# Scaling the attention output instead of its weights for four pairs, two compose tiles, an early second pair and six narrow FFN blocks

## Chip, core and metric

The kernel runs on one core of a Trainium2 chip. The metric is the device time of one execution in microseconds (us). TensorE (PE) multiplies matrices, VectorE (DVE), ScalarE (ACT) and GpSimd (POOL) work on elements, SyncE (SP) issues most transfers.

## What is computed

Three layers, one behind the other, on 2304 tokens of width 512:

```python
# attention, per head (4 batches, 8 heads, 576 tokens, head size 64)
decay = cum[:, :, :, None] - cum[:, :, None, :]      # cum = cumsum(log(clip(f)))
scores = where(causal, -1e9, q @ k.T / sqrt(D) + decay)
attn = exp(scores - max(scores)); attn = attn / (sum(attn) + 1e-9)
x = attn @ v
# FFN, float64 weights, d_ff 2048
h = x @ w_in
g = where(h >= 1, h, where(h <= -1, 0, (h + 1) ** 2 / 4))
x = g @ w_out
# top-1 mixture of 8 experts (d_ff 1024): gate by normalised dot products
out = gate * (max(x @ w1[e], 0) @ w2[e])
```

## The kernel before

**Order.** The instruction order of all engines is made when the program is built. Every step of the work is a Python generator that yields resources (`Buffers`), events and uses of an engine (`Use`, with a planned duration and a priority); `Order` plays these through and emits the instructions in the order that comes out. On the chip each engine then runs its own list strictly in order. What the plan got wrong in a duration shows on the chip as a wait.

**Attention.** Two heads make a pair, four pairs a batch, sixteen pairs in all. `load` brings q and k of a pair, VectorE transposes them (`turned`), and `unit` handles one of five query blocks (c = 4 is the last 64 queries of both heads in one block, then 3, 2, 1, 0): TensorE writes scores into a bank `SR` or `SRx`, VectorE adds the decay and the mask and takes the extreme (L588), ScalarE takes the exponential and its row sum (L593), VectorE turns the sum into its inverse (L598, L600), GpSimd scales P with it (L604), TensorE transposes P into a bank `T` (L618), ScalarE or VectorE copies that into `pt`, and `weighted` multiplies with v: the burst `X`, and `U` for the last 64 queries. For the first four pairs (`NSUM`) the decay comes from TensorE itself, by one more matmul (`sums`), and the mask from a fixed tile `past`; later pairs load a decay tile `cm`/`cl` for each pair, from a table `rows`. From pair 4 on `SRx` belongs to the FFN.

**Filler.** `keep_warm` issues matmuls of the identity (`warm`) wherever the plan has TensorE idle, until the first attention outputs are in place.

**FFN, first half.** The float64 weights arrive in 16 pieces of 512 KB (w_in and w_out in turn). `float64_piece` composes float32 values from the integer halves in a tile `wx` (one buffer): ScalarE absolute value, VectorE a maximum (L830), a shift (L832) and two merges (L834, L836), ScalarE the rounded high part, GpSimd the rest. The hidden layer is split into eight groups of 128; each takes twelve matmuls into a bank (`hp`, L886), then the activation, then twelve matmuls of the second layer (`accp`, L1020). Tokens go in blocks: `NARROW` = 5 blocks of 256, which start as soon as their attention pairs are there and mix with the rest of the attention, and then two blocks of 512. The second half of the FFN (`hr`) and the experts (`hm`) follow.

## Time and profile before

| | us |
|---|---|
| median of 3 runs | 861.24 (859.62 to 863.11) |
| profiled execution | 862.92 |
| its span, first to last instruction | 861.3 |

How to read it: the span is cut into stages, since the engines' shares change. TensorE is busy nearly throughout, but its filler counts as busy, so the filler's own records and the idle time per stage must be read with it. A lower granted clock (a share of full speed) marks stretches in which TensorE was slowed.

### The profile page before, as it was taken

The page shows a single profiled execution, that of the slowest core. Times are in us where ns is not written, and L with a number is a line of the kernel's source. Part 1 is how long each engine was busy: PE and PEld are TensorE (multiplying, and loading weights), DVE is VectorE, ACT ScalarE, POOL GpSimd, SP SyncE. Part 2 cuts the span into 40 slices and gives each one's busy share as a digit, 9 for nine tenths or more (in the row PEclk, how much of TensorE's full clock was granted, in tenths as well). Part 3 has the DMA queues.
Part 4 walks back from the last instruction along what each step waited for, and adds up shares of the span by engine and source line. Part 5 has one row for each costly group of instructions (what it writes and reads, how often), then busy time and mean ns, then how long its engine had stood idle before and what let it go on. Part 6 is the DMA issues. An engine that isn't in the chain of part 4 may idle for free.

```text
span 861.3 us, 14317 instructions
## 1 busy us (share of the span) xinstructions
PE 840.4 (98%) x5000; PEld 672.7 (78%) x5000; DVE 463.9 (54%) x1112; ACT 361.9 (42%) x845; POOL 306.4 (36%) x407
## 2 busy tenths in 40 slices
...
GB/s 139 184 183 182 167 159 145 139 135 108 113 67 118 78 103 134 74 75 171 117 127 49 73 123 159 189 191 123 147 123 73 50 50 50 263 103 50 98 74 25
DMA packets 152264, 101.91 MB, mean 118 GB/s; under 512 B 102866, under 2 KB 121810, under 8 KB 152192
## 3 DMA queue, kind: packets, MB, share of 16 engines
...
## 4 chain that ended last, share of the span: by engine, by line
PE 83%; DVE 7%; POOL 2%; issue 2%; DMA 2%; ACT 2%; SPq 0%; ACTq 0%; DVEq 0%; POOLq 0%
PE hm L886 12%; PE hr L886 12%; PE hp L886 9%; PE accp L1020 6%; PE accr L1020 6%; PE accBr L1020 6%; PE accm L1032 6%; PE accBm L1032 6%; PE SR L538 4%; PE T L618 4%; PE X L658 4%; PE gt L1236 1%; PE U L711 1%; PE SR L533 1%; PE T_None L618 1%
## 5 line engine op out<-in xcount | busy, mean ns | idle before, releaser
L908 POOL TENSOR_TENSOR glr<-gr,ghr 128x512 fp32r<-128x512 f32 x36 | 48.3, 1341 | 141.7 <-PE accBr L1020 69.1
L604 POOL TENSOR_SCALAR P<-P,st 128x512 f32<-128x512 f32 (+3 forms) x128 | 76.9, 615 | 38.8 <-DVE st L600 25.4
L886 PE MATMUL hr<-rx,wb 128*128 128x512 f32 (+1 forms) x384 | 90.1, 368 | 0.2 <-DVE rx L872 0.2
L886 PE MATMUL hm<-mx,wm 128*128 128x512 f32 (+1 forms) x336 | 87.0, 379 | 0.0
L593 ACT ACTIVATE P<-P,st 128x512 f32<-128x512 f32 (+3 forms) x128 | 71.4, 559 | 32.9 <-DVE st L588 31.8
L917 DVE SCALAR_TENSOR_TENSOR glm<-hm,ghm 128x512 fp32r<-128x512 f32 x36 | 24.8, 689 | 103.5 <-PE accBm L1032 68.4
L916 ACT ACTIVATE ghm<-hm 128x512 fp32r<-128x512 f32 x36 | 21.6, 599 | 132.9 <-PE accBm L1032 120.6
L886 PEld LDWEIGHTS hr<-rx,wb 128*128 128x128 f32 x384 | 65.5, 188 | 14.0 <-DVE rx L872 0.6
L886 PEld LDWEIGHTS hm<-mx,wm 128*128 128x128 f32 x336 | 61.0, 188 | 14.9 <-issue 3.4
L908 POOL TENSOR_TENSOR glp<-gp,ghp 128x512 fp32r<-128x512 f32 x36 | 49.8, 1383 | 55.1 <-ACT ghp L907 48.2
L1020 PE MATMUL accp<-ghp,wa 128*128 128x256 f32 (+1 forms) x384 | 68.8, 307 | 0.0
L588 DVE CUSTOM_DVE_ANT_0 P<-SR,cm 128x512 f32<-128x512 f32 (+3 forms) x96 | 45.1, 484 | 24.8 <-PE SR L538 22.5
L1020 PEld LDWEIGHTS accp<-ghp,wa 128*128 128x128 f32 x384 | 53.9, 190 | 5.3 <-issue 2.2
L618 PE MATMUL T<-ident,P 128*128 128x128 f32 x320 | 52.5, 278 | 3.5 <-POOL P L604 2.9
L638 ACT COPY pt<-T 128x512 f32<-128x512 f32 (+2 forms) x96 | 35.3, 391 | 35.9 <-PE T L618 35.2
L902 DVE SCALAR_TENSOR_TENSOR gr<-tr 128x512 f32<-128x512 f32 x36 | 25.9, 721 | 42.6 <-POOL glr L908 31.7
L618 PEld LDWEIGHTS T<-ident,P 128*128 128x128 f32 x320 | 36.7, 141 | 14.9 <-POOL P L604 6.5
L538 PE MATMUL SR<-kt,qt 64*128 64x384 f32 (+3 forms) x224 | 44.9, 478 | 3.0 <-DVE st L588 2.9
L1020 PE MATMUL accr<-ghr,wb 128*128 128x512 f32 (+1 forms) x160 | 47.0, 375 | 0.0
L1020 PE MATMUL accBr<-ghr,wb 128*128 128x512 f32 (+1 forms) x160 | 46.5, 372 | 0.0
L1032 PE MATMUL accm<-wm,ghm 128*128 128x512 f32 x144 | 46.2, 394 | 0.0
L1032 PE MATMUL accBm<-wm,ghm 128*128 128x512 f32 x144 | 45.8, 392 | 0.0
...
## 6 DMA issues: line engine op xcount, KB each, us to landing
...
```

The costliest lines, as they stand in the source:

```text
L538: nc.tensor.matmul(bank[:, j, :w], qt[p, P * c:P * c + P], kt[p, :w], start=True, stop=i >= NSUM)
L588: yield dve(w + 80, lambda: nc.vector.tensor_tensor_reduce(out=pv_, in0=so, in1=m, scale=-0.125, scalar=3e38, op0=ALU.add, op1=ALU.min, ac ...
L593: yield act(w, lambda: nc.scalar.activation(pw, pw, AF.Exp, bias=st[:, n:n + 1], scale=-1.0, accum_out=st[:, 2 + n:3 + n]), 1, 330)
L604: yield pool1(w, lambda: nc.gpsimd.tensor_scalar(pw, pw, st[:, 6 + n:7 + n], 1.0, ALU.mult, ALU.mult), 0)
L618: nc.tensor.transpose(T[:, P * n:P * n + P], p[:, P * kb:P * kb + P], ident)
L638: yield act(n, lambda: nc.scalar.copy(dh, src), 0)
L658: nc.tensor.matmul(X[D * j:D * j + D, P * kb:], vt[:, kb, j], pt[i, j][0][:, 512 * kb:512 * kb + 512 - P * kb], start=(kb == 0), stop=(kb ...
L886: nc.tensor.matmul(oo, a[:, c, cs], x[c], start=(ip == 0 and c == 0), stop=(ip == 2 and c == KC - 1))
L902: yield dve(n, lambda: nc.vector.scalar_tensor_tensor(g, t, 0.5, t, ALU.min, ALU.mult), 2)
L908: yield pool2(n, lambda: nc.gpsimd.tensor_tensor(gl, g, f32(gh), ALU.subtract), 1)
L1020: nc.tensor.matmul(acc[d][:, :w], b[:, fc, P * d:P * d + P], g, start=(fc == 0 and ip == 0 and (not narrow or d % 2 == 0)), stop=(fc == NF ...
L1032: nc.tensor.matmul(acc[a * (4 // na)], g[:, P * a:P * a + P], b[:, fc], start=(fc == 0 and ip == 0), stop=(fc == NF - 1 and ip == 2))
```

## The change

For the first four pairs P isn't scaled for the query blocks 3 to 0. The row sums of a pair go into one tile `tot` of 128 x 8. Once all eight are there, the new `shares` takes the inverse on VectorE and TensorE spreads it by eight matmuls with the identity into a bank R (the FFN's hidden bank, free at that time), laid out as X is. ScalarE copies R, and VectorE multiplies X with it into `xT`. Block 4 is scaled as before.

The compose tile gets two buffers until all 16 pieces are through (the second one lies in the attention's pool), and the maximum of the first nine pieces goes to GpSimd. The loads of the second pair no longer wait for the running sum. `NARROW` is 6, so the first FFN half has six blocks of 256, one of 512 and one of 256 in the wide layout.

```diff
+NMAX = 9
-    NARROW = 5
+    NARROW = 6
     FIRST = [(TB * n, TB) for n in range(NARROW)] + [
-        (t, 2 * TB) for t in range(TB * NARROW, NT, 2 * TB)]
+        (t, min(2 * TB, NT - t)) for t in range(TB * NARROW, NT, 2 * TB)]
...
-        if i:
+        if i == 1:
+            yield raw_ok[0, "k"]
+        elif i:
             yield sums_there
-        t = yield dma(P * S * 6, lambda: put({"q": q, "k": k}[n], n), 4 if i else 0.5, k=4)
+        t = yield dma(P * S * 6, lambda: put({"q": q, "k": k}[n], n),
+                      4 if i > 1 else 0.5, k=4)
...
+        late_sum = i < NSUM and c < 4
+        total = sums_of[i][:, c, n:n + 1] if late_sum else st[:, 2 + n:3 + n]
         yield act(w, lambda: nc.scalar.activation(pw, pw, AF.Exp, bias=st[:, n:n + 1], scale=-1.0,
-                                                  accum_out=st[:, 2 + n:3 + n]), 1, 330)
+                                                  accum_out=total), 1, 330)
         done(summed)
-        if n == 0:
+        if late_sum:
+            done(all_summed[i])
+        elif n == 0:
...
-        yield pool1(w, lambda: nc.gpsimd.tensor_scalar(pw, pw, st[:, 6 + n:7 + n], 1.0, ALU.mult,
-                                                       ALU.mult), 0)
+        if not late_sum:
+            yield pool1(w, lambda: nc.gpsimd.tensor_scalar(pw, pw, st[:, 6 + n:7 + n], 1.0,
+                                                           ALU.mult, ALU.mult), 0)
...
+    def shares(i):
+        yield all_summed[i]
+        tot = sums_of[i].rearrange("p c j -> p (c j)")
+        inv = ap.tile([P, 4, 2], F32, tag="inv", name=f"inv{i}", bufs=2)
+        yield Use("DVE", 150, lambda: nc.vector.tensor_scalar(tot, tot, 1e-9, None, ALU.add), 0)
+        yield Use("DVE", 150, lambda: nc.vector.reciprocal(inv.rearrange("p c j -> p (c j)"), tot), 0)
+        gh_ = yield (h_b, 1)
+        R = hidden_bank(f"R{i}", 0)
+        def spread():
+            for c in range(4):
+                for j in range(2):
+                    nc.tensor.matmul(R[D * j:D * j + D, P * c:P * c + P],
+                                     inv[:, c, j:j + 1].to_broadcast([P, D]), ident,
+                                     start=True, stop=True)
+        yield Use("PE", mm(P, 8), spread, 0.9)
...
-        yield act(512, lambda: nc.scalar.copy(xT[:, :512], X), 0)
+        if i < NSUM:
+            yield share[i]
+            R, gh_ = share[i].t
+            yield act(512, lambda: nc.scalar.copy(xT[:, :512], R), 0)
+            give(h_b, gh_)
+            yield dve(512, lambda: nc.vector.tensor_tensor(xT[:, :512], X, xT[:, :512], ALU.mult), 0)
+        else:
+            yield act(512, lambda: nc.scalar.copy(xT[:, :512], X), 0)
...
-        x = fp.tile([P, DM], I32, tag="wx", name=name + "x", bufs=1)
+        x = (ap if gx[0] else fp).tile([P, DM], I32, tag="wx", name=name + "x", bufs=1)
         yield act(DM, lambda: nc.scalar.activation(f32(x), f32(hw), AF.Abs), prio)
-        yield dve(DM, lambda: nc.vector.tensor_scalar(f32(x), f32(x), MIN64, None, ALU.max), prio,
-                  True)
+        if name == "wa" and len(early_max) < NMAX:
+            early_max.append(0)
+            yield Use("POOL", 1500, lambda: nc.gpsimd.tensor_scalar(
+                f32(x), f32(x), MIN64, None, ALU.max), prio)
+        else:
+            yield dve(DM, lambda: nc.vector.tensor_scalar(f32(x), f32(x), MIN64, None, ALU.max),
+                      prio, True)
```

`wx_b` grows from one buffer to two, and a new `one_tile` takes the second one back when all 16 pieces are done. `first_out` and `keep_first` take the block's own width.

The plan is made anew, so the order of all engines changes. Three places of it follow.

SP, the first loads behind those of the first pair (`war` is a weight piece, `rawq` and `rawk` are q and k, `rows` is the table of running sums). Before:

```order
L820 DMA war<-in_moe_w_in_dram 128x4x128
L820 DMA war<-in_moe_w_out_dram 128x512
L373 DMA rows<-cum 32x576
L420 DMA rawv_201<-in_v_dram 128x4x64 x2
L422 DMA rawv_201<-in_v_dram 64x2x64
L420 DMA rawv_212<-in_v_dram 128x4x64 x2
L422 DMA rawv_212<-in_v_dram 64x2x64
L400 DMA rawq_224<-in_q_dram 32x18x32 x4
```

and after:

```order
L863 DMA war<-in_moe_w_in_dram 128x4x128
L402 DMA rawq_166<-in_q_dram 32x18x32 x4
L402 DMA rawk_184<-in_k_dram 32x18x32 x4
L375 DMA rows<-cum 32x576
L425 DMA rawv_210<-in_v_dram 128x4x64 x2
L427 DMA rawv_210<-in_v_dram 64x2x64
L425 DMA rawv_222<-in_v_dram 128x4x64 x2
L427 DMA rawv_222<-in_v_dram 64x2x64
L863 DMA war<-in_moe_w_out_dram 128x512
```

The q and k of the second pair moved ahead of the `rows` store, and the second weight piece behind the loads of v.

VectorE, pair 4, between the reduces of its query blocks 3 and 2 (`P_13`, `P_02`; `wax` is the compose tile). Before:

```order
L588 ISA P_13_1090,st_3_1088<-SR,cm_932 128x512
L588 ISA st_3_1088 128x1
L832 TENSOR_SCALAR wax<-wax 128x512
L834 SCALAR_TENSOR_TENSOR wax<-war,wax 128x512
L588 ISA P_02_1115,st_2_1114<-SR,cm_932 128x384
L588 ISA st_2_1114 128x1
```

and after:

```order
L595 ISA P_13_1063,st_3_1061<-SR,cm_902 128x512
L595 ISA st_3_1061 128x1
L880 TENSOR_SCALAR wax<-wax 128x512
L882 SCALAR_TENSOR_TENSOR wax<-war,wax 128x512
L609 TENSOR_SCALAR st_3_1061<-st_3_1061 128x2
L884 SCALAR_TENSOR_TENSOR wax<-war,wax 128x512
L611 RECIPROCAL st_3_1061<-st_3_1061 128x2
L704 TENSOR_TENSOR xT_802<-X_1043,xT_802 128x512
L595 ISA P_02_1097,st_2_1096<-SR,cm_902 128x384
```

The product that scales pair 3's output came in, and a weight piece ends here; in the whole of this pair four pieces stand where one and a half stood.

TensorE, the end of pair 6's scores and the first scores of pair 7 (`SR<-kt,qz`, 128x288). Before:

```order
L618 MATMUL T_120_1770<-ident,P_12_1703 128x128 x3
L538 MATMUL SR<-kt_945,qt_944 128x128 x2
L533 MATMUL SR<-kt_1227,qz_86 128x288 x2
L886 MATMUL hp_6_1647<-px0h,wa_96 128x256 x4
L886 MATMUL hp_6_1647<-px0l,wa_96 128x256 x4
L886 MATMUL hp_6_1647<-px0h,wa_97 128x256 x4
L618 MATMUL T_010_1823<-ident,P_01_1753 128x128 x2
```

and after:

```order
L1068 MATMUL accp_1326<-ghp_6_1673,wa_98 128x256 x4
L1068 MATMUL accp_1326<-ghp_6_1673,wa_99 128x256 x4
L1068 MATMUL accp_1326<-glp_6_1674,wa_98 128x256 x4
L543 MATMUL SR<-kt_921,qt_920 128x128 x2
L752 MATMUL U_1797<-pu_1558,rawv_1444 64x64 x10
L630 MATMUL T_020_1839<-ident,P_02_1747 128x128 x3
L538 MATMUL SR<-kt_1269,qz_86 128x288 x2
L934 MATMUL hp_2_1802<-px1h,wa_96 128x256 x4
L934 MATMUL hp_2_1802<-px1l,wa_96 128x256 x4
L934 MATMUL hp_2_1802<-px1h,wa_97 128x256 x4
```

Before, these scores come ahead of the first block's last hidden group; after, that block's second layer is at its end and the second block's hidden groups have begun. Over the whole program TensorE has 88 `warm` instructions before and 67 after.

## Rows read from the trace of the kernel before

**Rows 1.** The page, busy time of TensorE and its weight loads, share and instructions.

```profile
PE 840.4 (98%) x5000; PEld 672.7 (78%) x5000; DVE 463.9 (54%) x1112; ACT 361.9 (42%) x845; POOL 306.4 (36%) x407
```

**Rows 2.** Busy time by window: length, PE, PEld, DVE, ACT, POOL, granted clock, DMA share, GB/s.

```profile
10.00:36.00 26.00, 25.72 (x182) 18.07 (x183) 19.62 (x53) 16.97 (x40) 10.72 (x17) 1.00 0.77 141
36.00:54.00 18.00, 16.62 (x121) 10.31 (x117) 16.96 (x59) 14.14 (x40) 10.64 (x17) 1.00 0.98 179
54.00:68.00 14.00, 12.90 (x95) 8.07 (x93) 12.50 (x40) 10.71 (x30) 10.38 (x15) 1.00 1.01 197
68.00:83.00 15.00, 13.19 (x105) 9.01 (x103) 11.90 (x35) 10.92 (x30) 10.24 (x17) 1.00 0.75 174
83.00:103.00 20.00, 19.57 (x159) 15.09 (x155) 17.48 (x46) 14.05 (x39) 14.20 (x23) 1.00 0.76 187
...
126.00:142.00 16.00, 12.48 (x84) 8.64 (x82) 13.23 (x35) 9.28 (x26) 10.22 (x17) 0.89 0.68 160
142.00:320.00 178.00, 177.37 (x1428) 141.27 (x1425) 100.40 (x324) 104.64 (x280) 91.99 (x159) 1.00 0.41 105
```

**Rows 3.** TensorE's waits, 0 to 90 us: line, waited for, total, times, longest.

```profile
PE T L618 <- POOL P L604: 2.9, 6, 0.8
```

**Rows 4.** Timeline of TensorE at 43 and 133 us: start, length, instruction, idle before.

```profile
43.01 1.24 PE L533 MATMUL SRx<-kt,qz 128*128 128x288 f32 x4
44.09 0.60 PE L618 MATMUL T<-ident,P 128*128 128x128 f32 x4
...
132.78 2.29 PE L533 MATMUL SR<-kt,qz 128*128 128x288 f32 x4 [0.99 <-DVE st L588]
134.45 1.47 PE L886 MATMUL hp<-px0h,wa 128*128 128x256 f32 x4
135.72 0.77 PE L886 MATMUL hp<-px0l,wa 128*128 128x256 f32 x4
```

**Rows 5.** Timeline of TensorE, the first filler.

```profile
1.52 8.78 PE L735 MATMUL warm<-ident 128*128 128x128 f32 x56 [1.52 <-POOL ident masks.py:199]
```

**Rows 6.** Timeline of TensorE, the X burst of pair 5.

```profile
124.02 2.37 PE L658 MATMUL X<-pt,rawv 128*64 128x512 f32 x16
```

**Rows 7.** SP's waits, 0 to 140 us, the `rows` store.

```profile
SPq L373 <- DVE cum L371: 5.4, 1, 5.4
```

**Rows 8.** Timeline of TensorE, dense FFN groups of 256 and of 512 columns.

```profile
322.84 1.12 PE L1020 MATMUL accp<-ghp,wa 128*128 128x256 f32 x8
...
324.28 1.12 PE L1020 MATMUL accp<-ghp,wa 128*128 128x256 f32 x8
...
346.22 2.93 PE L886 MATMUL hp<-px,wa 128*128 128x512 f32 x12
348.98 0.63 PE L1020 MATMUL accp<-ghp,wa 128*128 128x512 f32 x2
```

**Rows 9.** Timeline of VectorE, the last merge of a weight piece.

```profile
131.16 0.69 DVE L836 SCALAR_TENSOR_TENSOR wax<-war,wax 128x512 int32<-128x512 int32 x1
```

**Rows 10.** VectorE's groups by shape, 0 to 125 us: busy us, mean ns, idle before.

```profile
L836 DVE SCALAR_TENSOR_TENSOR wax<-war,wax 128x512 int32<-128x512 int32 x14 | 10.8, 768 | 0.2
L834 DVE SCALAR_TENSOR_TENSOR wax<-war,wax 128x512 int32<-128x512 int32 x14 | 10.0, 716 | 0.1
L598 DVE TENSOR_SCALAR st<-st 128x2 f32<-128x2 f32 x25 | 9.4, 376 | 1.1 <-ACT P L593 1.1
...
L830 DVE TENSOR_SCALAR wax<-wax 128x512 f32<-128x512 f32 x14 | 6.9, 491 | 0.7 <-ACT wax L829 0.7
L832 DVE TENSOR_SCALAR wax<-wax 128x512 int32<-128x512 int32 x14 | 6.9, 491 | 0.1
...
L598 DVE TENSOR_SCALAR st<-st 128x1 f32<-128x1 f32 x7 | 1.0, 144 | 2.0 <-ACT P_None L593 2.0
```

**Rows 11.** Timeline of VectorE, the first reduces of pairs 4 and 5.

```profile
79.51 0.76 DVE L588 CUSTOM_DVE_ANT_0 P_None<-SR,cl 128x576 f32<-128x576 f32 x1 [0.77 <-POOL cl L488]
...
96.62 0.74 DVE L588 CUSTOM_DVE_ANT_0 P_None<-SR,cl 128x576 f32<-128x576 f32 x1
```

30 lines of the change are left out of this document (22 added, 8 removed).

## Prediction

> **What bounds the kernel now.** I read the page's busy times first, then busy time by stage, then what TensorE waits for, then the rows around the holes.
>
> TensorE counts as busy for 98% of the span [rows 1]. That is not 98% useful. While the first attention pairs run, the plan fills its holes with matmuls of the identity (`warm`) that nobody reads. Taking window length minus PE busy, stage by stage [rows 2]: the front from 10 to 103 us leaves TensorE idle for 0.28 + 1.38 + 1.10 + 1.81 + 0.43 = 5.0 us, the stretch from 126 to 142 us for 3.5 us, and the 178 us after it for 0.6 us. So from 142 us on there is nothing to win but work taken off TensorE. Everything the change can gain lies ahead of that point, in three places: the filler, the 5.0 us of waits in the front, and the hole at 126 to 142.
>
> The hole costs more than its idle time. Its window alone has a granted clock of 0.89 [rows 2]. Four score matmuls of 288 columns that start at 132.78 take 1.67 us to the next start where they elsewhere take 1.08 (43.01 to 44.09), and the four FFN matmuls behind them 1.27 us where four of 256 columns take 0.48 in a dense stretch (a third of the 1.44 that twelve take from 322.84 to 324.28) [rows 4, 8]. That is 0.6 + 0.8 = 1.4 us at the lower of the two clock levels, after a stretch in which the engine had stood still between short groups. The hole is 3.5 + 1.4 = 4.9 us in all.
>
> **The change, part by part.** The terms are made against the profiled execution, 862.92 us with a span of 861.3.
>
> *Filler.* The order has 88 identity matmuls on TensorE before and 67 after. The first 28 take 8.78 us (each leaves two records) [rows 5], 0.31 us each. 21 fewer give 21 x 0.31 = **-6.6 us**. They are no free time by themselves: a filler that goes leaves a hole unless other work fills it, and that is the next term but one.
>
> *Output scaling.* For pairs 0 to 3 GpSimd no longer scales P (32 instructions leave), VectorE loses eight small instructions a pair and gains three (two small ones and one of 512 columns), ScalarE's copy reads R in place of X. New on TensorE: eight float32 matmuls a pair, 64 by 128 out, alternating between two halves of the columns. No row of before has these. The nearest is the X burst: eight instructions in the same two halves, 128 to 512 columns, 320 on average, in 2.37 us for all [rows 6]. By columns eight of 128 would be 2.37 x 128/320 = 0.9 us; by the filler's 0.31 each, 2.5 us. I take 1.5, nearer to the X rows because these have the same halves. Four pairs: **+6.0 us** (3.7 to 10). The chain behind X grows by one VectorE instruction in place of a ScalarE copy; R's copy runs while X is still being made, so I cost that at nothing, and at about 0.7 us for each of four pairs if R came last.
>
> *Early second pair, compose tiles, and the front's waits.* SP stands for 5.4 us ahead of its first `rows` store, waiting for VectorE's running sum [rows 7]. The second pair's q and k loads now stand in that gap; before they came behind it. Two compose tiles and nine maxima on GpSimd let weight pieces come earlier: the last piece's load stands ten places earlier on SP. T's waits for GpSimd's scaled P, 2.9 us [rows 3], have no cause left in the first four pairs. What is late next is ScalarE's exponential, one step up the same chain, and the VectorE reduce that frees the score bank. So I do not let the waits vanish: of 5.0 us I take **-2.0**, with both ends open, -5.0 if nothing new waits and +5.3 if VectorE becomes the bound (below). Behind every wait in the front stands the whole in-order TensorE queue.
>
> *The hole at 126 to 142.* In the order of before no FFN matmul stands between the pair-5 X burst and the first scores of pair 7: the FFN's last hidden group of the block needs the last piece of w_in, whose last VectorE step ends at 131.85 us, inside the hole [rows 9]. In the order after, hidden and second-layer matmuls stand there in groups of twelve. TensorE then has work while VectorE catches up. I take **-4.0** of 4.9 (0 to -4.9); what stays is that the decay tile of pair 7 still stands on SP behind the store of pair 5.
>
> *Six narrow blocks.* In the first FFN half 1344 - 960 = 384 matmuls of 256 columns replace 192 of 512. Twelve of 256 take 1.44 us (322.84 to 324.28), 0.120 each; twelve of 512 take 2.76 (346.22 to 348.98), 0.230 each [rows 8]. 384 x 0.120 - 192 x 0.230 = 46.1 - 44.2 = **+1.9 us**, 1 to 4 as the sixth narrow block mixes with attention, where groups are cut up. The last block of 256 leaves less work behind its last hidden group; I cost that at nothing, and at about 1 us if its second layer must wait for the GpSimd subtraction. The second half starts on the weight pieces that the plan paces from the end of attention; that has slack and no term.
>
> Sum: -6.6 + 6.0 - 2.0 - 4.0 + 1.9 = **-4.7 us**, 862.92 - 4.7 = 858.2. The profiled execution lies 1.7 us above the median of the runs shown (861.24), so I name 858.2 - 1.7 = **856.5 us**. The smallest change that a measurement of this kernel tells from none is about 0.5%, 4.3 us: faster means under 856.9, slower over 865.5.
>
> **Rivals.**
>
> *VectorE is freed further (B).* The two-column additions average 376 ns, the one-column ones 144 [rows 10]: VectorE stands in them for something that is not their size. If GpSimd's traffic is that cause, 32 scalings fewer let VectorE run ahead, all the front's waits go, and all of the hole: -6.6 + 5.0 - 5.0 - 4.9 + 1.9 = -9.6, 851.6 us. Against it: the nine maxima put work back on GpSimd, one beside each early piece. The Trainium skill, "SBUF — State Buffer", section "SBUF: two separate sides", says that VectorE and GpSimd share one pair of ports as an exclusive lock held for a whole instruction. By that rule the scalings that leave give this rival's time, and the moved maxima take part of it back. The 376 against 144 ns agree with it, but no row here names the cause.
>
> *VectorE becomes the bound at pair 4 (C), slower.* A weight piece costs VectorE 491 + 491 + 716 + 768 = 2466 ns [rows 10]. Between the first reduces of pairs 4 and 5, 79.51 to 96.62 us, 17.1 us apart [rows 11], the order of before has one and a half pieces, that of after four, none with its maximum moved (the nine are used up): 2.5 x 2.47 = 6.2 us more, plus 0.7 for the output product. TensorE has two more groups of twelve there, 24 x 0.125 = 3.0 us by the 0.120 above and a little mixing. If VectorE had no slack, TensorE would wait 3.9 us and pay 1.4 for the clock as at 132 us; with half of the hole's term left: -6.6 + 6.0 + 5.3 - 2.0 + 1.9 = +4.6, 865.8 us. It decides once that stretch exceeds 17.1 + 3.0 = 20.1 us. Against it: from 83 to 103 us VectorE is busy 17.5 of 20 us by durations that overlap [rows 2], so it has slack.
>
> *The change doesn't fill the hole (D).* If pair 7's decay tile sets the hole and the groups now standing there wait behind its scores, the term of 4.0 is lost: -0.7, 860.5 us.
>
> **How the numbers follow.** Forecast 0.50, B 0.22, C 0.16, D 0.12. The forecast's own spread is 854 to 860, about half of it under 856.9. Faster: 0.25 + 0.22 = 0.47. Slower: most of C and a rest, 0.15. Same: 0.38. The range from 851 to 864.5 takes in B's middle and D and leaves out C and the lower half of B, about 0.2.
>
> **What would show it.** The first `hp` matmul some 1 to 3 us earlier than before; no wait of T for GpSimd ahead of it; eight R matmuls in about 1.5 us; a clock of 1.00 and under 1 us of idle time from 120 to 150 us; the first FFN half about 2 us longer in matmuls. I am wrong if the front's idle time is over 8 us, if the granted clock falls in it now that fewer fillers stand there, or if the reduces of pairs 4 and 5 lie more than 20.1 us apart.

## The result: 870.3 us, 1.1% slower, and the profile after

| | before | changed |
|---|---|---|
| median, us | 860.43 | 870.32 |
| lowest and highest, us | 858.46, 863.11 | 869.35, 872.08 |
| ratio to before (95% interval) | 1 | 1.0108 (1.0081 to 1.0134) |
| profiled execution, us (span) | 862.92 (861.3) | 869.35 (867.7) |

The forecast was 856.5 us, with a range from 851.0 to 864.5 us. The time is outside it, on the slower side, and it differs from the time before by more than the 0.5% that can be told from no change.

The page's busy time of TensorE answers to [rows 1]. The share is 97%, a point lower:

```profile
PE 840.8 (97%) x5214; PEld 680.6 (78%) x5214; DVE 460.4 (53%) x1085; ACT 362.3 (42%) x847; POOL 297.0 (34%) x384
```

Busy time by window in the changed kernel, the same seven stretches as [rows 2] (window, its length, then PE, PEld, DVE, ACT and POOL busy with their counts, granted clock, DMA share, GB/s):

```profile
10.00:36.00 26.00, 25.11 (x183) 17.34 (x181) 21.64 (x57) 19.46 (x47) 12.72 (x13) 1.00 0.93 168
36.00:54.00 18.00, 15.94 (x126) 9.59 (x125) 15.29 (x38) 12.94 (x37) 9.53 (x11) 1.00 0.77 171
54.00:68.00 14.00, 12.49 (x100) 8.37 (x100) 12.20 (x34) 10.56 (x31) 9.40 (x11) 1.00 0.74 182
68.00:83.00 15.00, 13.44 (x117) 8.98 (x113) 13.26 (x37) 11.51 (x32) 7.32 (x11) 1.00 0.97 215
83.00:103.00 20.00, 16.14 (x133) 13.39 (x130) 17.06 (x41) 11.37 (x30) 12.58 (x16) 1.00 0.77 183
126.00:142.00 16.00, 16.00 (x128) 12.01 (x128) 8.87 (x36) 9.18 (x26) 8.57 (x17) 1.00 0.56 120
142.00:320.00 178.00, 176.13 (x1409) 139.32 (x1407) 101.16 (x328) 104.47 (x281) 90.91 (x162) 1.00 0.43 106
```

Length minus PE busy gives two readings. The hole at 126 to 142 us is gone, at full clock. The front, 10 to 103 us, stands idle for 0.89 + 2.06 + 1.51 + 1.56 + 3.86 = 9.9 us where it stood for 5.0. Who ended these waits (TensorE from 36 to 126 us; total, times, longest; compare [rows 3]):

```profile
PE T L630 <- ACT pt L650: 1.9, 2, 1.2
PE SR L538 <- DVE st L595: 1.8, 1, 1.8
PE hp L934 <- ACT tp L946: 1.7, 1, 1.7
PE SRx L543 <- DVE st L595: 1.5, 2, 1.3
PE T L630 <- DVE xT L758: 1.2, 1, 1.2
...
PE T L630 <- POOL P L616: 0.4, 1, 0.4
```

T hardly waits for GpSimd's scaled P any more, 0.4 us for 2.9. VectorE and ScalarE took that place. The longest single wait, 1.8 us, is that of scores whose bank a reduce of VectorE (`st`) has yet to free. One wait of that kind closely, in three timelines of the changed kernel (start, length, instruction, idle before). VectorE, the end of one reduce, a step of a weight piece, and the next reduce:

```profile
42.41 0.08 DVE L595 DVE_READ_ACCUMULATOR2_ANT st<- 128x1 f32 x1
42.77 1.49 DVE L880 TENSOR_SCALAR wax<-wax 128x512 int32<-128x512 int32 x1 [0.27 <-POOL wax L875]
44.18 0.28 DVE L595 CUSTOM_DVE_ANT_0 P<-SRx,past 128x128 f32<-128x128 f32 x1
44.38 0.08 DVE L595 DVE_READ_ACCUMULATOR2_ANT st<- 128x1 f32 x1
```

GpSimd, the maximum of the next piece and the subtraction of the piece before:

```profile
41.25 1.48 POOL L875 TENSOR_SCALAR wax<-wax 128x512 f32<-128x512 f32 x1 [4.36 <-ACT wax L872]
42.70 1.27 POOL L889 TENSOR_TENSOR wa<-wax,wa 128x512 fp32r<-128x512 f32 x1
```

TensorE, the scores that waited:

```profile
44.52 1.13 PE L543 MATMUL SRx<-kt,qt 64*128 64x512 f32 x4 [1.30 <-DVE st L595]
```

VectorE's L880 takes 0.41 us at its shortest and 0.47 at the median of sixteen pieces. Here it takes 1.49, and it starts 0.07 us behind a subtraction of GpSimd and ends 0.29 us after it. The reduce stands behind it in order, and TensorE behind the reduce. With one compose tile this pair of instructions can't meet: the subtraction reads the tile that the next piece needs.

Waits of TensorE at 62.97, 76.28 and 99.59 us (1.23, 1.20 and 1.80) stand behind VectorE steps that are stretched in the same way, each ending some 0.55 us behind a subtraction of GpSimd. With the one above that is 5.5 of the 9.0 us of idle time from 40 to 100 us. The longest stands behind a step of an FFN hidden group, 0.69 us at the median, and such a step can meet a subtraction with one tile too:

```profile
96.99 1.73 DVE L951 SCALAR_TENSOR_TENSOR gp<-tp,gp 128x512 f32<-128x512 f32 x1
```

A second cause is in ScalarE's queue. With the second tile its first step on a piece (L872) often stands there before the piece's load has landed, and whatever follows in ScalarE's order waits with it. ScalarE's waits from 10 to 126 us (the kernel before has none of this kind):

```profile
ACT wax L872 <- DMA war<-in_moe_w_in_dram: 5.2, 4, 2.4
ACT wax L872 <- DMA war<-in_moe_w_out_dram: 3.3, 4, 1.6
```

Two waits of TensorE, at 42.10 and 94.06 us (0.75 and 1.66), come straight behind one of these. The second, on ScalarE, VectorE and TensorE:

```profile
91.33 0.67 ACT L872 ACTIVATE wax<-war 128x512 f32<-128x512 f32 x1 [2.43 <-DMA war<-in_moe_w_in_dram]
92.03 0.43 DVE L878 TENSOR_SCALAR wax<-wax 128x512 f32<-128x512 f32 x1 [2.44 <-ACT wax L872]
94.06 0.74 PE L934 MATMUL hp<-px0h,wa 128*128 128x256 f32 x4 [1.66 <-ACT tp L946]
```

VectorE's first reduces of pairs 4 and 5, which answer to [rows 11], lie 25.5 us apart, where they lay 17.1:

```profile
78.02 0.76 DVE L595 CUSTOM_DVE_ANT_0 P_None<-SR,cl 128x576 f32<-128x576 f32 x1
...
103.48 0.72 DVE L595 CUSTOM_DVE_ANT_0 P_None<-SR,cl 128x576 f32<-128x576 f32 x1
```

So TensorE reaches its first `hp` matmul at 88.03 us, hardly earlier than the 88.33 of before, with 21 fillers fewer. The next loss lies far behind, where the second FFN half begins. TensorE's first `hr` matmuls and the first `accr` (before: 422.04 and 431.19 us, 9.15 apart; now 13.15):

```profile
425.08 0.73 PE L934 MATMUL hr<-rx,wb 128*128 128x512 f32 x2
427.79 0.50 PE L934 MATMUL hr<-rx,wb 128*128 128x512 f32 x1 [1.98 <-ACT rx L919]
428.87 0.76 PE L934 MATMUL hr<-rx,wb 128*128 128x512 f32 x1 [0.58 <-ACT rx L919]
...
438.23 0.63 PE L1068 MATMUL accr<-ghr,wb 128*128 128x512 f32 x2
```

They wait for ScalarE's conversion of the second half's first x block, which starts only at 424.13 us:

```profile
423.61 0.62 ACT L888 CAST wb<-wbx 128x512 fp32r<-128x512 f32 x1 [2.55 <-DVE wbx L884]
424.13 1.14 ACT L919 CAST rx<-rx 128x512 fp32r<-128x512 f32 x2
```

In the kernel before that conversion started at 418.06 us, 4 us ahead of the first `hr`. In the changed kernel the loads of x were issued from 410.33 us on and land 3.9 us later at the median, so x is not what is late on the chip. The conversion stands in ScalarE's order behind a weight piece of the second half (L888), and ScalarE is idle for 2.55 us until VectorE's last merge of that piece ends, which takes 1.67 us where 0.69 is the median, beside a subtraction of GpSimd that ends at 423.02:

```profile
421.91 1.67 DVE L884 SCALAR_TENSOR_TENSOR wbx<-wbr,wbx 128x512 int32<-128x512 int32 x1
```

From 425 to 445 us the granted clock is 0.91, 1.00 before.

The account between the two profiled executions, with durations of the changed one: fillers -6.6; four bursts of R +4.4; front idle 9.9 - 5.0 = +4.9; the hole -4.9; block list +1.9 in matmuls; two waits of `accp` for VectorE's copies of the narrow sums (`x_3b` 1.6 and `x_5b` 1.9) +3.5; start of the second half +4.0. That is +7.2 us. The last `accm` matmul ends at 858.7 us, before at 851.6: +7.1. By another cut TensorE's idle time from 10 to 850 us is 17.0 us against 10.3, and the lower clock costs the same in both; with -6.6, +4.4 and +1.9 that is +6.4, the difference of the two executions.

### The profile page after: what moved, and what is told of

Same layout as the page of the kernel before. It is cut to its first block, busy times and chain, and to the rows that moved or that the text cites. A ratio compares the mean times of both kernels' runs of the same rounds, so it can differ in the third digit from the quotient of the medians.

```text
span 867.7 us, 14684 instructions
## 1 busy us (share of the span) xinstructions
PE 840.8 (97%) x5214; PEld 680.6 (78%) x5214; DVE 460.4 (53%) x1085; ACT 362.3 (42%) x847; POOL 297.0 (34%) x384
## 4 chain that ended last, share of the span: by engine, by line
PE 84%; DVE 6%; DMA 4%; issue 2%; ACT 1%; SPq 1%; POOL 1%; ACTq 0%; DVEq 0%; POOLq 0%
PE hr L934 12%; PE hm L934 12%; PE hp L934 11%; PE accp L1068 9%; PE accr L1068 6%; PE accBr L1068 6%; PE accm L1080 6%; PE accBm L1080 6%; PE SR L543 4%; PE X L692 3%; PE T L630 3%; DMA war<-in_moe_w_in_dram 2%; PE accBp L1068 2%; PE gt L1285 1%; PE SR L538 1%
## 5 line engine op out<-in xcount | busy, mean ns | idle before, releaser
L1068 PE MATMUL accp<-ghp,wa 128*128 128x256 f32 (+1 forms) x448 | 75.0, 296 | 3.5 <-DVE x_5b L1111 1.9
L616 POOL TENSOR_SCALAR P<-P,st 128x512 f32<-128x512 f32 (+3 forms) x96 | 56.8, 604 | 35.1 <-DVE st L611 21.3
L1068 PEld LDWEIGHTS accp<-ghp,wa 128*128 128x128 f32 x448 | 61.2, 190 | 7.9 <-issue 2.2
L630 PEld LDWEIGHTS T<-ident,P 128*128 128x128 f32 x320 | 36.3, 140 | 14.6 <-issue 5.8
L950 DVE SCALAR_TENSOR_TENSOR gp<-tp 128x512 f32<-128x512 f32 x36 | 29.4, 817 | 31.2 <-ACT tp L946 18.6
```

The source lines that it names most:

```text
L616: yield pool1(w, lambda: nc.gpsimd.tensor_scalar(pw, pw, st[:, 6 + n:7 + n], 1.0, ALU.mult, ALU.mult), 0)
L630: nc.tensor.transpose(T[:, P * n:P * n + P], p[:, P * kb:P * kb + P], ident)
L950: yield dve(n, lambda: nc.vector.scalar_tensor_tensor(g, t, 0.5, t, ALU.min, ALU.mult), 2)
L1068: nc.tensor.matmul(acc[d][:, :w], b[:, fc, P * d:P * d + P], g, start=(fc == 0 and ip == 0 and (not narrow or d % 2 == 0)), stop=(fc == NF ...
```

## Experiments

Each kernel was timed beside runs of the kernel before. Diffs are against the changed kernel, where nothing else is said. "Against before" is (ratio - 1) times the median of before in the same runs; the changed kernel stands at +9.3 us by that, with an interval of 7.0 to 11.5; the others have 1.1 to 2.5 us to either side, so differences of 2 us between two kernels are not told from none.

Two sums over a profiled execution, both from 10 to 850 us, help to read the runs: TensorE's idle time, and an estimate of what the lower clock costs, the length times (1 - granted clock) added up over windows of 20 us (it costs that where TensorE is the limit). The first is 10.3 us in the kernel before and 17.0 in the changed one, the second 1.8 in both.

| kernel | us | ratio (95% interval) | against before, us |
|---|---|---|---|
| e1 last two blocks swapped | 870.57 | 1.0100 (1.0074 to 1.0127) | +8.6 |
| e2 early loads | 866.58 | 1.0053 (1.0033 to 1.0073) | +4.6 |
| e3 one tile | 864.87 | 1.0037 (1.0020 to 1.0053) | +3.2 |
| e4 no maxima on GpSimd | 871.93 | 1.0118 (1.0096 to 1.0140) | +10.2 |
| e5 five narrow blocks | 870.92 | 1.0110 (1.0094 to 1.0127) | +9.5 |
| e6 before, six narrow blocks | 865.06 | 1.0036 (1.0022 to 1.0050) | +3.1 |
| e7 no output scaling | 877.08 | 1.0166 (1.0151 to 1.0182) | +14.3 |
| e8 one tile and early loads | 862.52 | 1.0020 (1.0005 to 1.0034) | +1.7 |
| e9 pieces one behind another | 866.73 | 1.0062 (1.0042 to 1.0082) | +5.3 |
| e10 no early pair | 875.89 | 1.0170 (1.0148 to 1.0191) | +14.6 |
| e11 e8, six scaled pairs | 867.13 | 1.0066 (1.0048 to 1.0084) | +5.7 |
| e12 e8, five narrow blocks | 864.92 | 1.0054 (1.0033 to 1.0074) | +4.7 |
| p1 before, output scaling | 857.25 | 0.9950 (0.9936 to 0.9965) | -4.3 |
| p2 before, early pair | 861.87 | 1.0006 (0.9994 to 1.0019) | +0.5 |
| p3 before, both of these | 867.69 | 1.0069 (1.0053 to 1.0085) | +5.9 |
| p4 e8, no maxima on GpSimd | 865.12 | 1.0048 (1.0031 to 1.0065) | +4.1 |
| q1 p1, second tile and maxima | 882.48 | 1.0249 (1.0221 to 1.0278) | +21.4 |
| q2 before, second tile and maxima | 876.72 | 1.0172 (1.0144 to 1.0200) | +14.8 |

### The start of the second half: e1, e2, e6

e1 swaps the last two blocks of the first half, so that the block of 512 is last:

```diff
-        (t, min(2 * TB, NT - t)) for t in range(TB * NARROW, NT, 2 * TB)]
+        (TB * NARROW, TB), (TB * NARROW + TB, 2 * TB)]
```

> The changed kernel with the last two blocks of the first FFN half swapped: six blocks of 256 tokens, then one of 256 in the form of the wide blocks, then one of 512. The number of matmuls is the same. Theory T (transition): about 4 us are lost where the second half starts, because the second half loads and converts its first x block only when the first half has done its last hidden group, and behind a last block of 256 there is too little second-layer work (417.3 to 425.1 us from the last hp to the first hr, 12 us in the kernel before). With 512 last, 11 to 13 us lie there, the first accr comes 9 to 10 us behind the first hr (13.15 in the changed kernel, 9.15 in the kernel before), the clock of that stretch is 1.00, and the time is 870.3 - 4 = 866.3 us, 865.3 to 867.5. Rival W (weights): attention ends 13 us later in the changed kernel, the second half's weight pieces are paced from there, and they, not x, make the second half late. Then the 13 us stay and the time is 870 +- 1.2.

Measured 870.57 us: a miss, and the time that Rival W gives. From the last `hp` (419.57) to the first `hr` (431.69) lie 12.1 us as expected, and still `hr` waits, since ScalarE begins the conversions no earlier against it. The stage itself gains nothing: from the first wide `hp` to the last `accr` it takes 303.9 us, 303.8 in the changed kernel. They stand behind the last hidden group's own conversion, which came late in its turn (ScalarE of e1):

```profile
427.28 0.62 ACT L955 CAST ghp<-gp 128x512 fp32r<-128x512 f32 x1 [3.14 <-DVE gp L951]
427.81 1.13 ACT L919 CAST rx<-rx 128x512 fp32r<-128x512 f32 x2
...
429.41 0.60 ACT L919 CAST rx<-rx 128x512 fp32r<-128x512 f32 x1
```

So it isn't the length of the cover alone. e2 leaves the blocks and changes only when the second half's loads are let go:

```diff
+    def next_loads():
+        yield half0.x_ok[len(FIRST) - 1]
+        go(half1.loads())
...
+        go(next_loads())
         yield half0.first_done
...
-        go(half1.loads())
```

> The changed kernel with one thing added: the loads of the second half's x blocks are let go when the first half's last x block is there, and no longer when its last hidden group is done. The block order stays (512, then 256 last). Theory T: the first hr finds x converted, the first accr comes 9 to 10 us behind the first hr, and the time is 866.3 us, 865.3 to 867.5. Rival W (the second half's weight pieces are late): 13 us stay between the first hr and the first accr, 870 +- 1.2. If e1 gains and this one doesn't, the cover that the last block gives counts for another thing than x.

Measured 866.58 us, 4.7 us better than the changed kernel against before. The conversions run from 402.66 us on, and TensorE has no wait from 420 to 450 us. The expected distance from first `hr` to first `accr` is no measure here, since `hr` now starts among the last `accp` groups (423.9 and 443.5 us). From the first wide `hp` to the last `accr` it is 299.2 us, in the changed kernel 303.8. Rival W falls as it was put, since nothing was changed on the weights' pace. A weight piece has a part all the same: it is what ScalarE stood for ahead of x in the changed kernel, and e2 puts the conversions in front of it.

e6 sets the new block list into the kernel before, with the same edits of `FIRST`, `NARROW`, `first_out` and `keep_first` as the change:

```diff
-    NARROW = 5
+    NARROW = 6
...
-        (t, 2 * TB) for t in range(TB * NARROW, NT, 2 * TB)]
+        (t, min(2 * TB, NT - t)) for t in range(TB * NARROW, NT, 2 * TB)]
```

> The kernel before with the block list alone changed: six narrow blocks, one of 512 and one of 256 tokens. By the same three sizes the time is 861 + 7.8 = 868.8 us, 867 to 870, with 12 to 13 us from the first hr to the first accr; the front and the hole at 126 to 142 us stay as they are in the kernel before. Rival F: only the matmuls cost, 861 + 1.9 = 863, 862 to 864.5.

Measured 865.06 us, +3.1: between the two. The first `hr` comes at 422.1 us as before. That is a net, and what the narrow blocks cost ahead of it can't be read from it: the first `hp` comes 2.0 us earlier, and the window from 126 to 142 us has 4.9 us of idle time at a clock of 0.82, before 3.5 at 0.89. Then the first `accr` comes at 434.6, 12.5 us behind `hr` instead of 9.15. The loss shows at that place (TensorE's waits in e6 from 420 to 450 us; from 425 to 445 its granted clock is 0.91):

```profile
PE hr L886 <- DVE rx L872: 1.0, 1, 1.0
PE hr L886 <- ACT rx L871: 0.7, 2, 0.5
```

The waits for `x_5b` that I had added to the expectation don't occur in it.

### The front: e3, e4, e9

e3 takes the second tile away and keeps GpSimd's maxima:

```diff
-        Buffers(2), Buffers(2), Buffers(1), Buffers(1), Buffers(1), Buffers(1), Buffers(1), Buffers(2), Buffers(0))
+        Buffers(2), Buffers(1), Buffers(1), Buffers(1), Buffers(1), Buffers(1), Buffers(1), Buffers(2), Buffers(0))
...
-        go(one_tile())
```

> The changed kernel with a single compose tile, the nine maxima still on GpSimd. Theory P (front): with two tiles VectorE's steps on one piece run beside GpSimd's subtraction of the piece before, which stretches them to 1.1 to 1.5 us from 0.42 and 0.68, and the reduces that free the score banks come late; with one tile the subtraction must end before the next piece begins. Then VectorE's compose steps keep 0.42 to 0.75 us, PE's idle time from 40 to 100 us falls from 9.0 to 4 to 6 us, and the time is 866.5 us if the hole at 126 to 142 stays filled, 870 if it comes back. Rival Q (the front is late because VectorE has more to do in it, or the output scaling's chain is longer): the idle time from 40 to 100 us stays at 8 to 10 us, and the time is 870 to 875, since the pieces come later.

Measured 864.87 us. Busy time of TensorE by window in e3 (first numbers after the window: its length, PE busy):

```profile
40.00:60.00 20.00, 19.17 (x157) 12.57 (x157) 14.69 (x44) 15.75 (x48) 11.28 (x13) 1.00 0.93 182
60.00:80.00 20.00, 19.67 (x164) 12.79 (x164) 15.30 (x49) 15.60 (x44) 11.99 (x16) 1.00 0.90 200
80.00:100.00 20.00, 19.12 (x156) 16.34 (x154) 16.14 (x44) 12.02 (x32) 16.59 (x22) 1.00 0.64 145
100.00:126.00 26.00, 23.55 (x182) 16.10 (x182) 20.62 (x54) 16.85 (x43) 16.96 (x25) 1.00 0.75 185
126.00:142.00 16.00, 12.22 (x80) 8.52 (x78) 13.60 (x40) 10.13 (x27) 10.97 (x18) 1.00 0.60 144
```

The front's idle time from 40 to 100 us falls from 9.0 to 2.0, the first `hp` comes at 81.0 us, and the hole at 126 is back with 3.8 us: the pieces now come later. What VectorE's compose steps spend above their usual length between 36 and 103 us (steps over it by 0.15 us or more) falls from 6.7 to 2.4 us. This agrees with overlap, but also with fewer pieces early (6.5 ahead of the first reduce of pair 4 in VectorE's order, 10 in the changed kernel; the expectations of e9 and q1 count pairs 4 and 5 as 5 and 6), and with ScalarE's waits for the pieces' loads, which fall from 8.5 to 2.0 us.

e4 keeps both tiles and puts the maxima back on VectorE:

```diff
-NMAX = 9
+NMAX = 0
```

> The changed kernel with all maxima of the weight pieces on VectorE, two compose tiles kept (the plan then has 78 fillers, 67 in the changed kernel, which is 11 x 0.31 = 3.4 us). Theory P (two tiles let the subtraction overlap VectorE's steps): the stretched compose steps stay, PE's idle time from 40 to 100 us stays at 7 to 10 us, the time is 870 to 874 us. Rival M (it is the maxima on GpSimd, 1.53 us each with a hand-over from ScalarE and on to VectorE, that stretch or delay VectorE): idle time there falls to 4 to 6 us and the time is 866 to 868.

Measured 871.93 us. The idle time from 40 to 100 us is 5.5 us, as rival M had it, and the time is Theory P's: eleven fillers more stand in the front, and the granted clock is 0.91 from 60 to 80 us. No gain, so the maxima by themselves aren't what makes the changed kernel slow. From 10 to 850 us its idle time is 12.6 us, 4.4 less than in the changed kernel, and the lower clock costs 3.4 us more.

e9 keeps both tiles and the pieces early, and plans VectorE's steps on a piece behind the subtraction of the one before:

```diff
+        if name == "wa":
+            if lasts:
+                yield lasts[-1]
+            lasts.append(ok)
         yield dve(DM, lambda: nc.vector.tensor_scalar(
             x, x, 3, 0x3FFFFFFF, ALU.logical_shift_left, ALU.bitwise_and), prio, True)
```

> The changed kernel, two compose tiles kept, but VectorE's last three steps on a piece are planned only when the piece before is whole, GpSimd's subtraction included. The pieces stay early: 9 of them stand ahead of the first reduce of pair 5 on VectorE and 13.5 ahead of that of pair 6, where the changed kernel has 10 and 14 and the single tile 6.5 and 9. So it tells two readings of the single tile's gain apart. Theory P (overlap): VectorE's steps are stretched because the subtraction runs beside them. Then the time that compose steps spend above their usual length between 36 and 103 us falls from 6.7 us to under 3, PE's idle time from 40 to 100 us from 9.0 to 3 to 5 us, and the time is 864 to 866.5 us. Rival V (amount): VectorE has too many pieces early, overlap or not. Then the idle time stays at 7 to 10 us and the time is 869 to 873.

Measured 866.73 us. The stretch of the compose steps falls to 3.1 us and the idle time from 40 to 100 us to 6.4, not to 3 to 5. It is 4.0 us better than the changed kernel against before, so overlap is very likely a cause. It is not the only one: the early pieces stay, ScalarE still waits 9.7 us for their loads, and no run takes those waits away alone. By the two sums above, e9 has 1.7 us less idle time than the changed kernel and no loss to the clock. Among the runs with two tiles the stretch doesn't rank the times either: 3.4 us in e7 and 4.4 in q2, which are both slower than the changed kernel. The Trainium skill, "SBUF — State Buffer", section "SBUF: two separate sides", says that a VectorE operation with two SBUF inputs or in a two-port mode and a GpSimd operation that reads SBUF hold their shared ports as an exclusive lock for a whole instruction. The steps with two inputs, 1.73 us for 0.69 with the end 0.55 us behind GpSimd's, agree with that. L880 has one input, and no run here shows in which mode it ran; nor does one separate the ports from another resource of the two engines.

### The changed kernel with one part undone: e5, e7, e10

e5 goes back to five narrow blocks:

```diff
-    NARROW = 6
+    NARROW = 5
```

> The changed kernel with five narrow blocks and two of 512 tokens, as in the kernel before; all else stays changed. If the block list costs what the trace says (1.9 us of matmuls, 1.9 us of waiting of accp for the copy x_5b, 4 us at the start of the second half), the time is 870.3 - 7.8 = 862.5 us, 861 to 864, and the first accr comes 9 to 10 us behind the first hr. Rival F (nearly all is lost in the front, whose idle time from 40 to 100 us is 9.0 us where it was 5.0, and the later milestones only carry it on): 866 to 869 us.

Measured 870.92 us: no gain, and both theories miss. The start of the second half is cured (8.4 us from first `hr` to first `accr`), but now the first wide block waits. In the changed kernel attention ends at 325.5 us, in the kernel before at 312.5; a wide block's x is read when attention is done, and with five narrow blocks TensorE wants it at 332 us (its waits from 325 to 400 us in e5):

```profile
PE hp L934 <- ACT px L919: 3.2, 3, 1.2
PE accp L1068 <- DVE x_0b L1118: 1.8, 1, 1.8
```

From 330 to 400 us it is idle for 6.1 us. The sixth narrow block covers that, and its price comes at the end of the half. e5's lower clock costs 5.2 us, 1.8 in the changed kernel.

e7 leaves the output scaling out, so GpSimd scales P for all pairs:

```diff
-        late_sum = i < NSUM and c < 4
+        late_sum = False
...
-        if i < NSUM:
-            go(shares(i))
...
-        if i < NSUM:
+        if False:
             yield share[i]
```

> The changed kernel with GpSimd scaling P for all pairs again, and without the R matmuls; two compose tiles, GpSimd's maxima, the early pair and six narrow blocks stay. The plan then holds 79 fillers, 67 in the changed kernel. The sum: 12 x 0.31 = +3.7 us of filler, -4.1 us of R matmuls, and some T waits for GpSimd's P come back (2.9 us in the kernel before, 0.4 in the changed one). Theory S (the output scaling is about even, the tiles are the front's trouble): idle time from 40 to 100 us stays at 8 us or more, time 870 to 873. Rival R (the longer chain behind X, ScalarE's copy of R and VectorE's product, makes the front wait): idle time falls to 5 to 6 us, time 866 to 868.

Measured 877.08 us, 5.0 us worse than the changed kernel against before; both theories miss on that side. T waits for GpSimd for 5.9 us in eight places from 36 to 142 us, and `T_None` for 1.6. The lower clock costs 8.6 us.

e10 loads the second pair behind the running sum again:

```diff
-        if i == 1:
-            yield raw_ok[0, "k"]
-        elif i:
+        if i:
             yield sums_there
...
-                      4 if i > 1 else 0.5, k=4)
+                      4 if i else 0.5, k=4)
```

> The changed kernel with the second pair's q and k loaded behind the running sum again, as before. The plan then holds 81 fillers, 67 in the changed kernel: 14 x 0.31 = 4.3 us. If the early pair took those away for good, the time is 870.3 + 4.3 = 874.6 us, 873 to 876. If the filler that leaves only turns into waits, as the front's idle time of 9.0 us suggests, it is 869 to 871.5, with 4 to 6 us of idle time from 40 to 100 us.

Measured 875.89 us, 5.3 us worse: the early pair pays in the changed kernel. The time is the one that the 14 fillers gave, but by chance in part. The idle time is what the other reading wanted, 5.0 us from 40 to 100 us, and from 10 to 850 us it is 3.8 us less than in the changed kernel. What the trace loses is clock, 12.2 us of it against 1.8: 0.74 is granted from 10 to 30 us, 0.91 from 50 to 70 and 0.88 from 110 to 130. It is no single execution: the runs have mean clocks of 0.983 to 0.989, those of the changed kernel 0.991 to 0.995.

### Repairs put together: e8, e11, e12, p4

e8 is the edits of e3 and e2 together:

```diff
-        go(one_tile())
...
+        go(next_loads())
         yield half0.first_done
...
-        go(half1.loads())
```

> The changed kernel with both repairs: a single compose tile, and the second half's x loads let go when the first half's last x block is there. If the front's loss and the loss at the start of the second half are two things, the gains add: 870.3 - 5.5 - 3.7 = 861.1 us, 859.5 to 862.5, PE idle under 3 us from 40 to 100 us and no wait of hr for rx. If they are one thing, seen twice, it is 864 to 866.

Measured 862.52 us, +1.7 of the changed kernel's +9.3; singly the repairs gave 6.1 and 4.7. More than either, less than the sum of 10.8: two things in the main. Whether they overlap isn't settled, since the 3.2 us lie within the intervals. There are 2.1 us of idle time from 40 to 100 us and no wait of `hr` for `rx`.

e11 scales the output of six pairs on top of that, with `i < NSUM` replaced in `late_sum` and its tile, in `shares` and in `weighted`:

```diff
+NSC = 6
...
-        late_sum = i < NSUM and c < 4
+        late_sum = i < NSC and c < 4
```

> Both repairs (single compose tile, early loads of the second half), and the output scaling for six pairs, not four. In the run with both repairs TensorE is idle for 8.6 us from 100 to 200 us, 5.9 of it in waits of T for GpSimd's scaled P of the pairs that are still scaled there. If GpSimd is the cause, 3 to 5 us of that go and two more bursts of R come, 2 x 1.0 us: 862.5 - 2 = 860.5, 859 to 862. Rival H: R takes the one hidden bank of the FFN, which from pair 4 on is in use, so hidden groups and R wait for each other, and it is 863 to 867.

Measured 867.13 us: the rival's time, but hardly its mechanism, for R waits only 0.4 us for the bank. From 100 to 126 us the idle time goes (2.5 to 0.0), but from 126 to 142 us it is 3.3 us at a clock of 0.79, in e8 3.8 at 1.00. The lower clock costs 6.8 us in e11 and 1.8 in e8, and that is about as large as the loss.

e12 is e8 with five narrow blocks:

```diff
-    NARROW = 6
+    NARROW = 5
```

> Both repairs and five narrow blocks. With the single tile attention ends at 313 us (325 in the changed kernel), and so the first wide block's x should be there in time, other than with five narrow blocks in the changed kernel, where TensorE was idle for 6.1 us from 330 to 400 us. Theory: the matmuls' 1.9 us go, 862.5 - 1.9 = 860.6 us, 859.5 to 862, and under 1 us of idle time from 330 to 400 us. Rival: the sixth narrow block is needed to cover the wide block's loads here too, 864 to 868.

Measured 864.92 us, with runs from 862.8 to 869.1: a miss, though only 2.0 us of idle time stand from 330 to 400 us, in waits for the copies `x_0b` and `x_1b`. What made it slower than e8 isn't settled.

p4 is e8 without GpSimd's maxima:

```diff
-NMAX = 9
+NMAX = 0
```

> The changed kernel with both repairs and without GpSimd's maxima (69 fillers in the plan, 62 with them). By the filler it is 7 x 0.31 = 2.2 us slower than the repaired kernel, 862.5 + 2.2 = 864.7, 863.5 to 866. If the maxima on GpSimd are what holds the hole from 126 to 142 us open (3.8 us idle, waits of T for GpSimd's P), it is 859 to 862.

Measured 865.12 us, in the range of the fillers: with one tile the maxima on GpSimd are worth 2.4 us. The match is not clean. p4 has 2.2 us less idle time than e8 and loses 3.4 us more to the clock.

### Each part alone, in the kernel before: p1, p2, p3, q2, q1

p1 is the change with all but the output scaling undone:

```diff
-NMAX = 9
+NMAX = 0
...
-    NARROW = 6
+    NARROW = 5
...
-        if i == 1:
-            yield raw_ok[0, "k"]
-        elif i:
+        if i:
...
-        Buffers(2), Buffers(2), Buffers(1), Buffers(1), Buffers(1), Buffers(1), Buffers(1), Buffers(2), Buffers(0))
+        Buffers(2), Buffers(1), Buffers(1), Buffers(1), Buffers(1), Buffers(1), Buffers(1), Buffers(2), Buffers(0))
...
-        go(one_tile())
```

> The kernel before with the output scaling of four pairs alone: one compose tile, no maxima on GpSimd, the second pair loaded late, five narrow blocks. The plan holds 66 fillers, 88 before: 22 x 0.31 = -6.8 us, and the R matmuls cost +4.1 us. Theory G (it gains by itself, since T no longer waits for GpSimd's P and nothing else gets late): -2.7 us and up to 3.2 us of T's waits, 861.4 - 4 = 857.4 us, 855.5 to 859.5. Rival N (it pays only where the second tile has loaded GpSimd and VectorE; here the filler that leaves turns into other waits): 860 to 863 us.

Measured 857.25 us, ratio 0.9950 (0.9936 to 0.9965): the expected value, and faster than both kernels. What it does is seen between 36 and 103 us, in the kernel before and in p1 (as above; POOL's busy time stands ahead of the clock):

```profile
36.00:103.00 67.00, 62.29 (x466) 42.49 (x462) 58.84 (x177) 49.83 (x137) 45.46 (x70) 1.00 0.87 184
```

```profile
36.00:103.00 67.00, 62.69 (x497) 42.97 (x494) 56.97 (x162) 50.17 (x137) 32.50 (x48) 1.00 0.87 193
```

GpSimd has 13 us less to do. TensorE's 31 records more are no more work: there are 22 records of filler less and 48 short ones of R, and all others are 425 against 420. The first `hp` comes 3.0 us earlier, at 85.30. The idle time from 10 to 850 us is as before, 10.1 us, and the 1.8 us of lower clock at the hole are gone. So the gain is filler that is no longer needed, less R, and the clock.

p2 is the early pair alone, so one tile as in e3, the edits of e7, and

```diff
-NMAX = 9
+NMAX = 0
...
-    NARROW = 6
+    NARROW = 5
```

> The kernel before with the second pair's q and k loaded in the gap ahead of the running sum, alone. The plan holds 72 fillers, 88 before: 16 x 0.31 = -5.0 us. Theory G: TensorE gets the second pair's work for it and the time falls by 3 to 5 us, 856.5 to 858.5. Rival N: the filler turns into waits, as T and the reduces cannot follow faster; 860 to 862.5 us, with the idle time from 20 to 100 us up by 3 us or more from 4.7.

Measured 861.87 us, no difference, and Rival N has it. But the time is not lost where the rival said: the first `hp` comes at 80.87 us, 7.5 us earlier, and the idle time from 20 to 100 us falls from 4.7 to 2.7 us. From 100 to 142 us TensorE is then idle for 8.6 us (before: 3.5), as T waits for GpSimd's P (8.0 us up to 142). What the front gains the hole takes.

p3 has both, scaling and early pair; against p1 it is

```diff
-        if i:
+        if i == 1:
+            yield raw_ok[0, "k"]
+        elif i:
             yield sums_there
```

> The kernel before with both, output scaling and early pair; one compose tile, no maxima on GpSimd, five narrow blocks, the second half's loads as before. 69 fillers in the plan. Theory G with gains that add: 861.4 - 4 - 3.5 = 854 us, 852 to 856.5. If they share one limit (only the number of fillers counts, 19 x 0.31 - 4.1 = -1.8, and VectorE's and GpSimd's pace): 857 to 860. Rival N: 860 to 863, a new wait taking all of it.

Measured 867.69 us, 10 us slower than the scaling alone; all theories miss. From 126 to 200 us, p3 and then p1:

```profile
126.00:142.00 16.00, 12.67 (x70) 7.27 (x70) 13.39 (x37) 9.27 (x26) 9.55 (x17) 0.89 0.51 117
142.00:200.00 58.00, 55.12 (x430) 42.81 (x428) 38.21 (x112) 35.50 (x95) 31.70 (x55) 0.97 0.55 124
```

```profile
126.00:142.00 16.00, 13.67 (x114) 8.56 (x114) 13.46 (x38) 10.26 (x29) 9.58 (x18) 1.00 0.68 155
142.00:200.00 58.00, 57.40 (x447) 45.62 (x446) 33.86 (x108) 34.35 (x95) 32.03 (x56) 1.00 0.51 114
```

p3 is idle for 3.3 us more there and has the lower clock; it loses 1.4 and 1.4 us in waits of `accp` for copies of narrow sums, and 2.5 us of idle time from 423 to 453 us, at the start of the second half, where p1 has 0.7 from 415 to 445. From 10 to 850 us that is 6.8 us of idle time and 3.4 us of clock more than p1, which is the whole difference of the two executions.

q2 is the second tile with the nine maxima alone, so the edits of e5, e7 and e10 together:

```diff
-    NARROW = 6
+    NARROW = 5
...
-        late_sum = i < NSUM and c < 4
+        late_sum = False
...
-                      4 if i > 1 else 0.5, k=4)
+                      4 if i else 0.5, k=4)
```

> The kernel before with the second compose tile and the nine maxima on GpSimd alone. The plan holds 89 fillers, 88 before. Theory P: the hole at 126 to 142 us goes (3.5 us idle and 1.4 of clock, -4.9), the front's waits grow by 5 us or more since GpSimd has the maxima on top of the scaling of P, and the time is 862 to 868 us. Rival E: the hole goes and the front stays as it is: 856 to 859 us.

Measured 876.72 us, +14.8: on Theory P's side, at twice its largest. The same window as above in q2:

```profile
36.00:103.00 67.00, 59.15 (x416) 40.69 (x415) 53.97 (x160) 45.83 (x125) 51.09 (x69) 0.92 0.81 190
```

GpSimd has 5.6 us more, TensorE issues 50 records fewer than before, and the clock falls to 0.92. The first `hp` comes at 96.58 us, 8.3 us late. Of the 16.5 us between the two profiled executions 10.3 are idle time and 5.0 the lower clock. Which of the two, tile or maxima, does it here wasn't tried; T waits for GpSimd for 5.4 us from 36 to 142 us. The window from 126 to 142 us is full, 16.00 of 16.00 us, as in the changed kernel, but the idle time stands ahead of it, where the kernel before has none:

```profile
100.00:126.00 26.00, 21.80 (x165) 16.83 (x163) 23.92 (x62) 16.71 (x47) 19.38 (x29) 1.00 0.54 138
```

q1 is p1 with the second tile and the maxima; against p1 it is

```diff
-NMAX = 0
+NMAX = 9
...
+        go(one_tile())
```

> The kernel with the output scaling alone (857.25 us), and on top of it the second compose tile with the nine maxima on GpSimd. The plan holds 81 fillers, 66 with scaling alone, 15 x 0.31 = 4.7 us, and 11 pieces ahead of pair 5 and 16 ahead of pair 6 on VectorE, 8 and 10 with scaling alone. Theory P (the tile loses by itself: VectorE's steps overlap GpSimd's subtraction and pieces crowd in front of the reduces): 857.25 + 4.7 and 2 to 5 us of front waits, 862 to 868 us, stretched compose steps of over 4 us in sum between 36 and 103. Rival E (the tile harms only with the early pair): it fills the hole at 126 to 142 us (2.3 us idle with scaling alone) and gives 855 to 859.

Measured 882.48 us, +21.4, the worst of all, 12.0 us of it lower clock by the sum above. Rival E falls: the tile, with the maxima, needs no early pair to do harm.

## Why the prediction was wrong, step by step

The parts alone give -4.3 (scaling), +0.5 (early pair), +3.1 (block list) and +14.8 (tile and maxima), +14.1 in sum; together they make +9.3. The last two were costed as a gain and as +1.9.

*Filler.* The count was right, 21 fewer, and they bought nothing ahead of the FFN: the first `hp` matmul came 0.3 us earlier, not 1 to 3. This sign was missed.

*Output scaling.* Sized at +6.0 us for R (rival B's sum took 5.0, without a reason); a burst takes 1.09 us in the trace (16 records at 32.72 us), 4.4 for four. I chose 1.5 between 0.9 and 2.5, and the X rows were the right ones alone. The larger mistake is that I saw its gain for the chain in front of T as a part of -2.0: by itself it is worth -4.3 us in all, the only part of the change that gains alone.

*Front waits.* This is the step that failed. I took -2.0 of 5.0 us; they grew by 4.9. I had named a growth, VectorE at pair 4 (rival C, chance 0.16), with its sign, reduces over 20.1 us apart. They are 25.5 apart, and from 83 to 103 us TensorE is idle for 3.9 us, the price that C had named; the clock stayed at 1.00. That the price is met is luck. C took VectorE to be without slack, but it was busy for 17.1 of the 20 us and stood idle for 2.4 of them in one piece. Of the 3.9 us, 1.8 are a wait for a reduce that stood behind one stretched step, and 1.7 a wait for ScalarE, which had stood for a piece's load. I argued against C with VectorE's slack, 17.5 busy of 20 us. That view counts what VectorE does, not what stands in a queue ahead of a reduce or a copy. And I had costed the second tile as a means to have pieces earlier. I never costed it as a wait removed between the subtraction and the next piece, which had kept VectorE and GpSimd apart (e3, e9), nor as a first step that stands in ScalarE's queue ahead of its load. That the tile does it is shown, by e3; how the loss divides between the stretch, the waits for loads and the number of early pieces is not.

*The hole.* Right: 4.9 us gone, idle 0.0, clock 1.00. But q2 closes it as well and loses 14.8 us. In every run with two tiles the window from 126 to 142 us has no idle time, in every run with one tile 2.3 to 4.9 us. So it is the tile that empties this window, and the gain was bought with the front's loss; it was no independent term. In part the hole only moves: from 100 to 126 us q2 is idle for 4.2 us, where the kernel before is idle for 0.0 and the changed one for 0.6.

*Six narrow blocks.* The +1.9 of matmuls can't be told apart in e6, whose first `hr` comes as before. The sentence on the last block failed: "I cost that at nothing, and at about 1 us if its second layer must wait for the GpSimd subtraction". It costs 3 to 5 us (e6 +3.1, e2 -4.7), by the conversions of the next half's x, which the plan lets go with the last hidden group of this half and which then stand late in ScalarE's order, in the changed kernel behind a weight piece. I had said of the second half only that its weight pieces have slack; neither x nor ScalarE's order was looked at. The short last block is one way into this loss and not the only one: with five narrow blocks the first `accr` comes 11.4 us behind the first `hr` in p3 and 15.1 in q1. The second price, 3.5 us of waits for the copies of narrow sums, had no term; e6 and e12 don't show such waits, p3 (2.8 us) and e11 (1.4) do, so they come with the mix of attention and narrow blocks and not with the sixth block alone.

*Range.* It was too narrow on the slower side by 5.8 us. C at its own price gave 865.8; with the start of the second half, +4.0, it would have been 869.8, near the measured time, but by a price that was met by luck.

What stays open: why the early pair costs 10 us on top of the scaling (p3 against p1) and saves 11.9 us when the tile is there too (e5 against q1), but 5.3 with six narrow blocks (the changed kernel against e10). First `hp` matmuls, weight pieces that the plan has on VectorE ahead of the first reduce of pair 5, and the two sums from 10 to 850 us (profiled executions):

| kernel | first `hp`, us | pieces | idle, us | clock, us | against before, us |
|---|---|---|---|---|---|
| before | 88.33 | 10 | 10.3 | 1.8 | 0 |
| p1 scaling | 85.30 | 10 | 10.1 | 0.0 | -4.3 |
| p2 early pair | 80.87 | 10 | 13.9 | 1.8 | +0.5 |
| p3 both | 84.00 | 9 | 16.9 | 3.4 | +5.9 |
| q2 tile, maxima | 96.58 | 15 | 20.7 | 6.8 | +14.8 |
| q1 p1, tile, maxima | 91.78 | 16 | 21.0 | 12.0 | +21.4 |
| e10 changed, no early pair | 94.96 | 16 | 13.2 | 12.2 | +14.6 |
| e5 changed, five blocks | 87.71 | 14 | 17.6 | 5.2 | +9.5 |
| changed | 88.03 | 14 | 17.0 | 1.8 | +9.3 |

So it is known where the time stands: in p3 it is two thirds idle time and one third clock, and 6.8 of the 11.9 us between q1 and e5 are clock. Why the waits fall as they do is not known. It looks as if attention and the pieces had to keep step, and as if the early pair (attention ahead) and the tile (pieces ahead) make up for each other in part. That is a reading of the table; no run varied the step alone, and q1 and e10, with equal pieces, lie 6.8 us apart.
